# An attention and MLP kernel on one core: some thirty words of a hand-written step table change places

## The chip, the cores and the metric

The kernel runs on one core of a Trainium2 chip. The metric is the device time of one execution in microseconds (us), as the median of three runs. A second number, the span, comes from one further execution that the hardware profiler recorded: it is the stretch from the first to the last instruction of the program in the trace.

## The reference

The input is q, k and v of shape (8 batches, 8 heads, 576 positions, 64), s of shape (8, 8, 576), a gain of 512 numbers and two weight matrices. Everything is float32 outside the kernel.

```python
cum = np.cumsum(np.maximum(s, 0.0), axis=-1)
bias = -(cum[:, :, :, None] - cum[:, :, None, :])
scores = np.where(causal, -1e9, scale * (q @ k.T) + np.minimum(bias, 0.0))
attn = softmax(scores)                     # over the last axis
x = (attn @ v)  ->  (batch, 576, 512)      # the heads side by side
xn = (x - mean(x)) / np.sqrt(var(x) + 1e-6) * g_ln
out = x + np.maximum(xn @ w_ch1, 0.0) @ w_ch2   # 512 -> 2048 -> 512
```

So there are eight batches of causal attention whose scores carry a decay bias, and behind each a layer norm and a two-layer MLP with a residual.

## The kernel before

**The table.** All of the work is done in `fast_path`. Its last part is a table of words, `PLAN` (line 1317), and a loop that takes the words one after the other, looks each up in the dictionary `STEPS` and calls the step, which emits its instructions. A word is a step's name, its arguments behind dots, and at times an engine behind a colon (A is ScalarE, D is VectorE, P is GpSimd). Each engine works off its own instructions strictly in the order in which the words emitted them, so the place of a word decides what an instruction stands behind on its engine. Words that go to different engines only wait for each other's data and buffers. DMAs are issued by an engine as well: those of SyncE (SP in the profile) go out on its hardware queue (q1), those of GpSimd (POOL), which cast float32 to bfloat16 on the way, on a software queue (q0). A GpSimd DMA uses one of eight semaphores in turn, so that issue n waits until DMA n-8 has landed.

**The work on TensorE (PE).** Batch 0 is done tile by tile. Batch 1 is done head by head: `s.8` to `s.15` are its scores (line 391), `v.8` to `v.15` its products with v (`pv`, line 590), where each word takes all five key blocks of one head. From batch 2 on two heads go together: `B2.n` (`burst`, line 553) makes the scores of pair n, `bx` their exponentials on ScalarE (line 560), `bm` the causal masks on GpSimd (`select`, line 497), and `Y` (`pv_two`, line 626) the products. The MLP of each batch is a queue of units from which `u` and `U` take the next one and put it between the attention: first the 16 units of the first layer (`ph`, line 792), then for each of four row tiles four quarters of the second layer (`py`, line 811), of which quarter i needs quarter i of the second weight matrix. Behind the fourth quarter the result goes out (`yo`, line 823, output DMA line 844).

**What is loaded where.** The names in the prediction are these:
- On GpSimd's queue: `w1.c` and `w2.i` load a quarter of the first and the second weights (lines 253 and 256, 512 KB each, tile `w_bf`). `lp.g` loads the k and the q of head pair g (`kp`, `qp`, line 184, 144 KB each); pair 7 is the last of batch 1, which has pairs 4 to 7, and pair 8 is the first of batch 2. `LV.b.t` loads a block of v (line 192, 128 KB, the last block 64 KB).
- On SyncE's queue: `lr.b.t` loads the rows of k and of q of a batch and row block as float32 (line 206, `rowtmp`, 256 KB each), `lv.b.t` the rows of v. `aug` and `a3` copy the bias rows into the key and query tiles of batches 0 and 1 (lines 265 and 267). `D` is the DMA that transposes the normed rows of batch 1 for its MLP (line 763), `Da.1.4` the one for the last, short row blocks of batches 0 and 1 (line 759), whose MLP units come at the very end of the queue, `tr` transposes k and q rows (line 225).
- On GpSimd's compute queue: `cr.b.t.u` casts a loaded row tile (line 218), `vm.b.t:P` multiplies v rows with the key weights (line 233), `vo` writes the weights' own columns (lines 245 and 246), `tk` copies the tail keys (line 145), `bm` are the masks.
- On TensorE and behind it: `Q` transposes a loaded pair (line 323) and `E` copies it out, `F` and `G` do so for the pairs of batch 2 (line 361), `l` is the last step of the layer norm of batch 1 (`xn`, line 741, VectorE).

The weight quarters, pairs and v blocks all stand in one row on GpSimd's queue. The rows for later batches stand in one row on SyncE's. The two queues use the same sixteen DMA engines of the core.

Of the kernel before, what the change touches and what calls it, by code (L numbers as in the profile page):

```python
# [16 lines left out]
P = 128  # L17
# [13 lines left out]
def fast_path(  # L31
# [13 lines left out]
    B, H, S, D = q.shape  # L45
# [13 lines left out]
    G = 4  # L59
# [896 lines left out]
    E = {"A": "act", "D": "dve", "P": "pool", "S": "sync"}  # L956
# [249 lines left out]
    def raise_flag(count, ones, n):  # L1206
# [113 lines left out]
        lc.k.3 lc.q.3 g LV.0.2 w1.0 LV.0.3 lp.4 cr2.0 cr2.1 fv.1 fk.0 fk.1 lc.k.4 lc.q.4 w1.1 f.7 f.8 fv.0 lp.5  # L1320
        w1.2 f.9 f.10 LV.1.0 LV.1.1 LV.1.2 LV.1.3 LV.1.4 lp.6 LV.0.4 w1.3 w2.0 lp.7 lp.8 w2.1 f.11 relu.0 scan.0
# [3 lines left out]
        x.1.1.0 T.2.1 e.2.0:D S.1.0.1 lr.3.0 lp.9 x.1.0.0 V.1.1 x.1.0.1 S.2.0.1 e.2.1:D S.2.0.2 S.2.1.2 T.3.0  # L1325
        S.2.1.1 N.1.1 S.2.0.0 L.0 V.1.0 x.2.0.1 x.2.0.2 x.2.1.2 X.0 e.3.0:D N.1.0 x.2.1.1 L.1 x.2.0.0 S.2.1.0
        S.3.0.2 B.0.1 T.3.1 B.1.0 x.2.1.0 e.3.1:D B.1.1 S.3.0.0 S.3.0.3 y.0:A aug x.3.0.2 V.2.0 M.0.0.0 x.3.0.3
        M.0.0.3 S.3.0.1 V.2.1 S.3.1.1 x.3.0.1 N.2.0 M.0.0.2 bc.4 S.3.1.3 x.3.0.0 X.1 x.3.1.3 y.1:A N.2.1 M.0.0.1
        S.3.1.2 V.3.0 S.3.1.0 M.0.1.3 L.2 T.4.0 M.0.1.0 r.0.0:A N.3.0 X.2 x.3.1.2 Q.q.4 x.3.1.0 x.3.1.1 e.4.0:D
        T.4.1 y.2:D M.0.1.2 Q.k.4 E.q.4.0:A B.3.0 E.k.4.0:A S.4.0.1 e.4.1:D S.4.1.0 M.0.1.1 E.q.4.1:D E.k.4.1:D  # L1330
        x.4.0.1 x.4.1.0 U A.1 V.3.1 s.8 N.3.1 u L.3 B.2.1 B.2.0 d.8 S.4.0.0 X.3 y.3:A r.0.1:D Q.q.5 E.q.5.1:A
        E.q.5.0:D S.4.1.1 x.4.1.1 x.4.0.0 Q.k.5 Sk u wr u u v.8 La.3 E.k.5.0:D B.3.1 n.8 B.0.0 U xk cr.3.0.0 a3
        lr.3.1 Q.k.6 E.k.6.0:A E.k.5.1:A u s.9 V.4.1 E.k.6.1:D N.4.1 M.0.2.3 M.0.2.2 V.4.0 Q.q.6 N.4.0 s.10 v.9
        A.3 qu.3 M.0.2.0 lp.11 d.10 A.2 M.0.2.1 E.q.6.0:D s.11 n.9 u Q.k.7 E.q.6.1:D w2.2 d.12 s.12 r.0.2:A
        E.k.7.0:D E.k.7.1:D O2.k.8:A v.10 n.10 Q.q.7 u s.13 E.q.7.0:D w2.3 E.q.7.1:D wT v.11 lp.10 u wx n.11
        ga.1.0.2 lv.2.0 A.0 u d.14 ga.1.0.0 v.12 qu.4 n.12 O2.k.9:A s.14 cr.3.1.0 ga.1.0.3 u F.k.8 v.13 u R qu.5
        n.13 La.6 F.k.9 ga.1.1.2 s.15 v.14 u G.k.9:D ga.1.1.0 n.14 U v.15 O2.q.8:A O2.q.9:A U n.15 F.q.9 qu.6
        lr.3.2 O2.k.11:A vo.2:P u ga.1.2.0 ga.1.2.1 ga.1.0.1 La.2 me cr.3.1.1 u l.0 O2.q.11:A F.q.8 U ga.1.1.3
# [280 lines left out]
```

## Time and profile before

| | us |
|---|---|
| median of three runs | 345.14 |
| lowest and highest of these | 344.15, 345.18 |
| the profiled execution's own time | 346.36 |
| its span | 344.9 |
| its time outside the span | 1.46 |
| PE busy | 331.5 (96% of the span) |
| VectorE, ScalarE, GpSimd busy | 199.5, 187.7, 168.6 |

The profile lists times in us from the start of the span. PE is TensorE's matmuls, DVE is VectorE, ACT is ScalarE, POOL is GpSimd, and SPq is the time in which SyncE issued a DMA. A row of the timeline gives the start, the duration, the engine, the line, the operation, what it writes and reads (tile names without their numbers), how many instructions the row holds, and in brackets how long the engine stood before it and what ended that. A row of the DMA view gives for each queue the number of packets, the MB moved and the share of the engines' time. TensorE was granted 0.991 of its full clock.

### The profile page before, as it was taken

Reading aid. Unit: us, or ns where it says so; the run is one execution under the profiler, and the core shown is the slowest. Engines: PE = TensorE matmul, PEld = TensorE weight load, DVE = VectorE, ACT = ScalarE, POOL = GpSimd, SP = SyncE. Lnnn points to the kernel's source line nnn. Section 1 sums busy time; section 2 is a strip of 40 time slices with the busy share of each in tenths; the row PEclk is TensorE's granted clock in tenths of the full one; section 3 lists DMA queues with packets and bytes.
Section 4 is the critical chain, followed back from the end, with each engine's and each line's share of the span. In section 5 each row is a group of like instructions: output and inputs, shape, how many; then the busy total and the mean of one; then the engine's idle time right before and its main releaser. Section 6 shows DMA issues by size and latency. Waiting matters only on the chain.

```text
span 344.9 us, 8061 instructions
## 1 busy us (share of the span) xinstructions
PE 331.5 (96%) x3117; PEld 183.3 (53%) x3117; DVE 199.5 (58%) x567; ACT 187.7 (54%) x348; POOL 168.6 (49%) x305
## 2 busy tenths in 40 slices
PE   6999989989998998999999999999999999999993
PEld 2899756545554554555555545554455444444443
DVE  6598777837685675347653664566448624523421
ACT  4998899677664675357736774486344204202200
POOL 8896768777377947683984377441301001000000
PEclk9899999999999999999999999999999999999998
DMA  9999999999999999999998966700510141020022
GB/s 144 181 189 177 172 193 195 214 208 233 164 215 227 169 245 195 216 228 198 205 209 205 214 108 151 139 2 2 121 63 2 24 129 46 3 90 33 2 62 65
DMA packets 147962, 48.59 MB, mean 141 GB/s; under 512 B 135280, under 2 KB 143760, under 8 KB 147920
## 3 DMA queue, kind: packets, MB, share of 16 engines
q1 hardware_dynamic: 121856, 38.34, 57.3%
q0 software_dynamic: 24304, 8.92, 22.0%
q10 hardware_dynamic: 1760, 0.79, 0.9%
q8 instruction: 25, 0.41, 0.5%
q14 instruction: 17, 0.14, 0.1%
HBM read 37.11 MB, written 9.44 MB: 135 GB/s over the span
## 4 chain that ended last, share of the span: by engine, by line
PE 77%; DMA 10%; POOL 7%; DVE 1%; issue 1%; SPq 1%; ACT 0%; POOLq 0%; DVEq 0%
PE py L811 34%; PE ph L792 31%; DMA v_bf<-in_v_dram 5%; PE pot L626 4%; DMA kp<-in_k_dram 3%; PE sa L553 2%; DMA rowtmp<-in_k_dram 2%; PE sb L553 1%; PE sc L553 1%; PE pott L664 1%; DMA rowtmp<-in_v_dram 1%; POOL rowb L180 1%; PE pot L590 1%; SPq L206 1%; POOL v_bf L233 1%
## 5 line engine op out<-in xcount | busy, mean ns | idle before, releaser
L811 PE MATMUL py<-w_bf,hT 128*128 128x512 bf16 (+2 forms) x608 | 131.1, 368 | 0.1
L792 PE MATMUL ph<-xT,w_bf 128*128 128x512 bf16 x480 | 109.8, 379 | 0.2 <-ACT er L560 0.2
L783 ACT ACTIVATE hT<-ph 128x512 bf16<-128x512 f32 x102 | 60.9, 604 | 77.6 <-PE ph L792 76.1
L811 PEld LDWEIGHTS <-hT 128*128 128x128 bf16 x608 | 55.9, 98 | 59.8
L792 PEld LDWEIGHTS <-w_bf 128*128 128x128 bf16 x544 | 51.3, 98 | 56.5 <-issue 0.3
L497 POOL TENSOR_SCALAR_AFFINE_SELECT er<-er 128x256 bf16<-128x256 bf16 x96 | 38.8, 419 | 48.7 <-ACT er L560 34.3
L823 DVE SCALAR_TENSOR_TENSOR yo<-py,rstd,xb 128x512 f32<-128x512 f32 x32 | 24.0, 751 | 50.5 <-PE py L811 46.2
L560 ACT ACTIVATE er<-sb 128x512 bf16<-128x512 f32 x48 | 28.2, 609 | 22.1 <-PE sb L553 17.9
L781 DVE TENSOR_SCALAR hT<-ph 128x512 bf16<-128x512 f32 x34 | 23.5, 691 | 27.5 <-PE ph L792 26.0
L233 POOL TENSOR_TENSOR v_bf<-rowtmp,wt 128x512 bf16<-128x512 f32 (+1 forms) x30 | 33.1, 1107 | 10.0 <-DMA rowtmp<-in_v_dram 9.8
L560 ACT ACTIVATE er<-sa 128x512 bf16<-128x512 f32 x48 | 28.6, 609 | 16.4 <-PE sa L553 15.1
L560 ACT ACTIVATE er<-sc 128x512 bf16<-128x512 f32 x48 | 28.8, 614 | 3.8 <-PE sc L553 3.8
L626 PEld LDWEIGHTS <-er 128*128 128x128 bf16 x480 | 19.8, 97 | 12.8 <-POOL er L497 4.0
L715 POOL TENSOR_TENSOR rstd<-rstd,mhalf 128x4 f32<-128x4 f32 (+1 forms) x8 | 8.7, 1093 | 34.3 <-DVE rstd L714 34.2
L626 PE MATMUL pot<-v_bf,er 128*128 128x66 bf16 x480 | 22.5, 193 | 3.1 <-POOL er L497 2.1
L700 DVE BATCH_NORM_STATS2 stats<-xb 128x6 f32<-128x128 f32 (+1 forms) x84 | 24.8, 326 | 0.6
L741 DVE SCALAR_TENSOR_TENSOR xn<-xb,mv,gb 128x512 bf16<-128x512 f32 x28 | 24.5, 874 | 1.0
L218 POOL CAST kq<-rowtmp 128x512 bf16<-128x512 f32 (+1 forms) x30 | 19.0, 645 | 12.2 <-DMA rowtmp<-in_k_dram 11.8
L643 DVE TENSOR_REDUCE sums<-pot 128x4 f32<-128x8 f32 x48 | 7.8, 163 | 29.5 <-PE pot L626 29.1
L645 DVE TENSOR_TENSOR xb<-pot,rinvs 128x256 f32<-128x256 f32 x48 | 20.4, 424 | 1.7
L553 PEld LDWEIGHTS <-kq 64*128 64x128 bf16 x384 | 11.9, 94 | 9.6 <-issue 4.2
L218 POOL CAST rowb<-rowtmp 128x512 bf16<-128x512 f32 (+1 forms) x20 | 12.8, 652 | 3.3 <-DMA rowtmp<-in_k_dram 2.9
(178 smaller groups left out, 393.2 us busy)
## 6 DMA issues: line engine op xcount, KB each, us to landing
out_dram<-yo SPq DMA_DIRECT2D x32, 256.0 KB
rowtmp<-in_v_dram SPq DMA_DIRECT2D x24, 256.0 KB
rowtmp<-in_k_dram SPq DMA_DIRECT2D x20, 256.0 KB
rowtmp<-in_q_dram SPq DMA_DIRECT2D x20, 256.0 KB
w_bf<-in_moe_w_ch_dram POOLq DMA_DIRECT2D x8, 512.0 KB, 9.0
kp<-in_k_dram POOLq DMA_DIRECT2D x8, 144.0 KB, 10.2
qp<-in_q_dram POOLq DMA_DIRECT2D x8, 144.0 KB, 10.2
v_bf<-in_v_dram POOLq DMA_DIRECT2D x8, 128.0 KB, 8.3
```

The lines of the kernel that those rows point to most:

```text
L218: nc.gpsimd.tensor_copy(out=rows[b % 2][0:pn, t, u], in_=loaded.pop(("kq"[u], b, t))[0:pn])
L233: e.tensor_tensor(out=v_bf[b % 2][0:pn, t, :, 0:D], in0=loaded.pop(("v", b, t))[0:pn], in1=wt[0:pn, t, b, :].unsqueeze(2).to_broadcast([pn ...
L497: nc.gpsimd.affine_select(out=out, in_=out, compare_op=ALU.is_ge, fill=0.0, base=0, pattern=pattern, channel_multiplier=-1,)
L553: nc.tensor.matmul(a, lhsT=lhsT, rhs=rhs, start=True, stop=True)
L560: nc.scalar.activation(out=er[:, 2 * n % 4 + i, o : o + 512], in_=bank["B", n].pop((name, i)), func=ACT.Exp, scale=scale,)
L626: nc.tensor.matmul(pot[:, t, :], lhsT=e[:, o : o + P], rhs=v_bf[b % 2][:, kb, h, :], start=(kb == 0), stop=(kb == t),)
L700: nc.vector.bn_stats(out=st[b][:, t, part, :], in_=x_tiles(b)[t][:, lo:hi])
L741: nc.vector.scalar_tensor_tensor(out=xn, in0=tiles[t], scalar=mvs[b][:, t, 0:1] if b > 0 else mean0[:, t : t + 1], in1=gb, op0=ALU.subtrac ...
L783: nc.scalar.activation(out=dst, in_=ph, func=ACT.Relu)
L792: nc.tensor.matmul(ph, lhsT=w1_bf[:, kd, fb * P : (fb + 1) * P], rhs=xT[:, :, kd, :], start=(kd == 0), stop=(kd == KD - 1),)
L811: nc.tensor.matmul(py[t], lhsT=hT[:, fb, t * P : (t + 1) * P], rhs=w2_bf[:, fb, c0:c1], start=(fb == 0), stop=(fb == FB - 1),)
L823: nc.vector.scalar_tensor_tensor(out=yo, in0=py[t], scalar=rs, in1=x[:, c0:c1], op0=ALU.mult, op1=ALU.add)
```

## The change

The table is written in another order. No word goes and none is new; one word, `r.0.2`, names VectorE instead of ScalarE. Nothing outside the table changes. The first rows that differ:

```diff
-        w1.2 f.9 f.10 LV.1.0 LV.1.1 LV.1.2 LV.1.3 LV.1.4 lp.6 LV.0.4 w1.3 w2.0 lp.7 lp.8 w2.1 f.11 relu.0 scan.0
+        f.9 f.10 LV.1.0 LV.1.1 LV.1.2 LV.1.3 fk.0 LV.1.4 lp.6 LV.0.4 lp.7 lp.8 w1.3 w2.0 f.11 relu.0 scan.0
...
-        B.0.0 U xk cr.3.0.0 a3
-        lr.3.1 Q.k.6 E.k.6.0:A E.k.5.1:A u s.9
+        B.0.0 U xk cr.3.0.0 lr.3.1 a3 Q.k.6 E.k.5.1:A E.k.6.0:A E.k.6.1:D u s.9
```

(The second pair is cut to the words around the move.) In the order of the program:

1. **GpSimd's loads.** `lp.7` and `lp.8` go ahead of `w1.3` and `w2.0`, and `w2.1` goes behind `lp.9`. A small memset (`fk.0`) goes behind `LV.1.3`.
2. **SyncE's first rows.** `lr.3.1` goes ahead of `a3`.
3. **Small steps between 30 and 62 us.** `E.k.5.1` goes ahead of `E.k.6.0` on ScalarE, `r.0.2` goes to VectorE, and `v.14` goes ahead of `s.15` on TensorE.
4. **Around the start of batch 2.** `lv.2.3` and `lv.2.4` go ahead of `lr.3.3`; `l.1` and `D` go back, `D` behind `lr.3.4` and a second output; `cr.3.0.1` and `cr.3.2.0` go ahead of `vo.3`; `vm.2.1` goes ahead of `tk.2`; `F.q.11`, `G.q.9` and `bx.9.2` go forward and `O2.k.10` back.
5. **Later.** `cr.4.1.0` goes behind the mask `bm.12.0`, `cr.5.1.0` and `cr.5.0.0` behind the mask `bm.16.2`; `Da.1.4` goes back behind `lr.5.2`; `lr.6.0` goes ahead of `lr.5.4`, and `lv.6.0` behind `lv.5.4`.

On SyncE, in the first fifteen of its DMAs, this is what changes (`kq_111` and `kq_110` are the key and query tiles of batches 0 and 1 that get the bias rows, from `aug` and `a3`):

```order
 L265 DMA kq_111<-c_122 1x4x576
 L267 DMA kq_111<-c_122 1x4x576 x3
+L206 DMA rowtmp<-in_k_dram 128x8x64
+L206 DMA rowtmp<-in_q_dram 128x8x64
 L265 DMA kq_110<-c_122 1x4x576
 L267 DMA kq_110<-c_122 1x4x576 x3
-L206 DMA rowtmp<-in_k_dram 128x8x64
-L206 DMA rowtmp<-in_q_dram 128x8x64
 L206 DMA rowtmp<-in_v_dram 128x8x64
```

The two row loads of `lr.3.1` now stand ahead of the four copies of `a3`.

On GpSimd, in the row of its early loads, the pairs and the weights change places (the first pair of the piece is pair 7, the second pair 8; line 253 is `w1.3`, the first row of line 256 is `w2.0`):

```order
 L192 DMA v_bf_107<-in_v_dram 64x8x64
-L253 DMA w_bf<-in_moe_w_ch_dram 128x4x512
-L256 DMA w_bf<-in_moe_w_ch_dram 128x4x512
-L184 DMA kp<-in_k_dram 96x2x384
-L184 DMA qp<-in_q_dram 96x2x384
-L184 DMA kp<-in_k_dram 96x2x384
-L184 DMA qp<-in_q_dram 96x2x384
+L184 DMA kp<-in_k_dram 96x2x384
+L184 DMA qp<-in_q_dram 96x2x384
+L184 DMA kp<-in_k_dram 96x2x384
+L184 DMA qp<-in_q_dram 96x2x384
+L253 DMA w_bf<-in_moe_w_ch_dram 128x4x512
```

Four loads of 144 KB now stand ahead of two of 512 KB; the row that follows, line 256, is `w2.0` in both.

On GpSimd again, at the first pair of batch 4 (`er` are the exponentials that the masks cut, `kq_111` takes the cast rows of batch 5, `v_bf` the weighted v rows):

```order
 L233 TENSOR_TENSOR v_bf_107<-rowtmp,wt 64x8x64
-L497 AFFINE_SELECT er<-er 128x2x128 x3
-L218 CAST kq_111<-rowtmp 128x512 x2
-L497 AFFINE_SELECT er<-er 128x2x128
-L218 CAST kq_111<-rowtmp 128x512 x2
+L497 AFFINE_SELECT er<-er 128x2x128 x4
+L218 CAST kq_111<-rowtmp 128x512 x4
 L233 TENSOR_TENSOR v_bf_108<-rowtmp,wt 128x8x64
```

The fourth mask (`bm.16.2`) no longer stands behind two casts.

More of the change, by code (lines that the diff above doesn't have):

```diff
@@ L1324, in fast_path @@
         V.0.1 N.0.1 tc.2 e.1.0:A S.1.0.0 e.1.1:A S.1.1.1 x.0.0.0 x.1.1.1 qu.2 V.0.0 S.1.1.0 bc.2 T.2.0 N.0.0
[L1325 to L1338, printed above, removed]
@@ new lines, in fast_path @@
+        S.2.1.0 S.3.0.2 B.0.1 T.3.1 B.1.0 x.2.1.0 e.3.1:D B.1.1 S.3.0.0 S.3.0.3 y.0:A aug x.3.0.2 V.2.0 M.0.0.0
+        x.3.0.3 M.0.0.3 S.3.0.1 V.2.1 S.3.1.1 x.3.0.1 N.2.0 M.0.0.2 bc.4 S.3.1.3 x.3.0.0 X.1 x.3.1.3 N.2.1
+        M.0.0.1 y.1:A S.3.1.2 V.3.0 S.3.1.0 M.0.1.3 L.2 T.4.0 M.0.1.0 r.0.0:A N.3.0 X.2 x.3.1.2 Q.q.4 x.3.1.0
+        x.3.1.1 e.4.0:D T.4.1 y.2:D M.0.1.2 Q.k.4 E.q.4.0:A B.3.0 E.k.4.0:A S.4.0.1 e.4.1:D S.4.1.0 M.0.1.1
+        E.q.4.1:D E.k.4.1:D x.4.0.1 x.4.1.0 U A.1 V.3.1 s.8 N.3.1 u L.3 B.2.1 B.2.0 d.8 S.4.0.0 X.3 y.3:A
@@ new lines, in fast_path @@
+        u F.k.8 v.13 u R qu.5 n.13 La.6 F.k.9 ga.1.1.2 v.14 s.15 u G.k.9:D ga.1.1.0 n.14 U v.15 O2.q.8:A
+        O2.q.9:A U n.15 F.q.9 qu.6 lr.3.2 O2.k.11:A vo.2:P u ga.1.2.0 ga.1.2.1 ga.1.0.1 La.2 me cr.3.1.1 u l.0
+        O2.q.11:A F.q.8 U ga.1.1.3 ga.1.1.1 lv.2.1 lv.2.2 G.k.8:A ga.1.2.2 vm.2.0:P ga.1.2.3 lv.2.3 lv.2.4
+        lr.3.3 F.q.11 l.3 F.k.11 u G.q.9:A cr.3.0.1 l.2 G.q.8:A cr.3.2.0 vo.3:P G.k.11:A G.q.11:D lr.3.4 u U
+        O2.k.10:A l.1 D F.k.10 U O2.q.10:A G.k.10:A F.q.10 vm.2.1:P to G.q.10:A u lv.3.0 U lr.4.0 tk.2 B2.8
@@ new lines, in fast_path @@
+        vm.2.2:P bx.8.3 u bx.8.1 vm.2.3:P sd.2 bx.8.4 vm.2.4:P bx.8.2 qu.7 se.2 u bx.8.5 sm.2 ga.1.0.4 u bx.8.0
+        bm.8.3 u bm.8.1 B2.9 bx.9.2 bm.8.2 bm.8.0 bx.9.5 Y.8.1 ga.1.1.4 lr.4.1 cr.3.2.1 bx.9.4 cr.3.3.0 bx.9.0
+        Y.8.0 cr.3.3.1 K.8.0 tr.3.0.2 bm.9.3 cr.3.4.1 K.8.1 bm.9.0 bx.9.3 bx.9.1 bm.9.1 u bm.9.2 U u u Y.9.0
+        vm.3.0:P ga.1.2.4 la.1.4 B2.10 bx.10.0 K.9.0 bx.10.3 bx.10.4 bx.10.2 bx.10.5 cr.3.4.0 bm.10.3 bx.10.1
+        Y.9.1 U K.9.1 u tr.3.2.4 u U u lv.3.1 tr.3.4.5 bm.10.1 Y.10.1 bm.10.0 B2.11 bx.11.0 bx.11.4 lv.3.2
@@ new lines, in fast_path @@
+        bx.11.5 lv.3.3 K.10.1 bm.10.2 Y.10.0 K.10.0 bm.11.2 ga.2.0.0 lv.3.4 bx.11.2 bm.11.0 La.4 bx.11.1 u
+        ga.2.1.2 ga.2.0.3 U u cr.4.1.1 lr.4.2 bx.11.3 Y.11.0 K.11.0 bm.11.3 u U bm.11.1 u ga.2.0.1 lr.4.3
+        cr.4.0.1 vm.3.1:P Y.11.1 K.11.1 lv.4.0 lv.4.1 tk.3 vm.3.4:P lr.4.4 u ga.2.1.0 u Z.2 z.2 B2.12 bx.12.0
+        vm.3.2:P U bx.12.4 bm.12.2 ga.2.1.1 bx.12.1 lv.4.2 ga.2.2.0 cr.4.2.1 ga.2.2.1 ga.2.1.3 lv.4.3 la.2.0
+        la.2.1 cr.4.0.0 bx.12.5 bm.12.3 vm.3.3:P ga.2.2.2 bx.12.3 bm.12.1 u bx.12.2 bm.12.0 cr.4.1.0 u u sd.3
@@ new lines, in fast_path @@
+        se.3 u B2.13 bx.13.5 bx.13.1 ga.2.0.2 la.2.2 u bx.13.0 cr.4.4.0 sm.3 u bx.13.4 ga.2.2.3 u la.2.3 Da.2.0
+        bx.13.3 u Y.12.0 bx.13.2 bm.13.0 K.12.0 u u B2.14 cr.4.4.1 tr.4.4.5 bx.14.2 Y.12.1 K.12.1 bx.14.1
+        bm.13.2 bx.14.3 vo.4:P bx.14.4 u u u tr.4.0.2 bx.14.5 bm.13.1 bm.13.3 bx.14.0 Y.13.0 B2.15 bx.15.0
+        K.13.0 bx.15.2 cr.4.3.1 cr.4.2.0 cr.4.3.0 tr.4.2.4 u lr.5.0 u vm.4.1:P Y.13.1 bx.15.3 bx.15.5 bx.15.1 u
+        K.13.1 bx.15.4 bm.14.1 bm.14.2 bm.15.0 tk.4 ga.3.0.0 U U bm.14.0 u bm.15.1 Y.14.0 K.14.0 bm.14.3 Y.14.1
@@ new lines, in fast_path @@
+        cr.5.4.0 u cr.5.4.1 bx.17.2 bx.17.3 bm.17.0 la.3.1 la.3.2 la.3.3 cr.5.2.0 bm.17.1 tr.5.4.5 bx.17.5
+        bm.17.3 lr.6.1 u u qm u u cr.5.3.1 u cr.5.2.1 u tk.5 vo.5:P cr.6.1.1 Da.3.0 u u lv.5.4 Y.17.0 lv.6.0
+        B2.18 bx.18.3 bx.18.2 bx.18.0 K.17.0 bx.18.1 u u Y.17.1 K.17.1 bx.18.4 bx.18.5 bm.18.3 tr.5.2.4 u u
+        ga.3.1.4 ga.3.0.4 B2.19 bx.19.0 vm.5.3:P bx.19.3 bm.18.2 ga.4.0.1 bm.18.1 cr.5.0.1 bm.18.0 tr.5.0.2
+        vm.5.0:P bx.19.1 u bm.19.1 u u lv.6.1 sd.5 u bx.19.5 se.5 Y.18.1 sm.5 K.18.1 u vm.5.1:P Y.18.0 ga.3.2.4
@@ new lines, in fast_path @@
+        u la.5.3 Da.5.0 cr.7.3.1 bm.25.1 u u u u cr.7.2.0 B2.26 bx.26.3 bm.25.0 vm.7.2:P bx.26.4 Y.25.0 bx.26.2
+        K.25.0 cr.7.2.1 bx.26.1 bm.26.2 u u u bm.25.3 Y.25.1 bx.26.0 bx.26.5 K.25.1 ga.6.0.0 vm.7.3:P bm.26.0
+        B2.27 bx.27.0 u tk.7 bx.27.4 sd.7 bx.27.3 bm.27.2 bx.27.5 u ga.6.0.3 u bm.26.3 bm.26.1 se.7 la.5.4
+        tr.7.2.4 u u U Y.26.1 u U sm.7 bx.27.1 bm.27.1 Da.5.4 Y.26.0 K.26.0 bm.27.3 K.26.1 ga.6.1.2 bx.27.2
+        bm.27.0 vm.7.4:P ga.6.1.3 u vm.7.1:P u u Y.27.0 K.27.0 ga.6.1.0 Z.6 z.6 B2.28 bx.28.0 ga.6.0.2 bx.28.1
@@ new lines, in fast_path @@
+        bm.30.1 U u U bm.30.3 bx.31.1 bm.31.1 Y.30.1 K.30.1 ga.7.1.0 bm.31.3 ga.7.1.3 bx.31.4 bm.31.2 u U Y.31.1
+        K.31.1 U bm.31.0 ga.7.1.2 u Y.31.0 K.31.0 u Z.7 z.7 ga.7.2.2 ga.7.2.3 ga.7.2.0 u ga.7.0.4 ga.7.1.4
+        ga.7.2.4 ga.7.1.1 u u u U ga.7.0.0 u u u u la.7.0 ga.7.2.1 la.7.1 la.7.2 la.7.3 Da.7.0 u u u u u u u u u
+        u u u u u u u u U u U u la.7.4 U u U u u u u U U gd u Da.7.4 u u u u u u u u u u u u u u u u U u u u U U
+        U u u U u U U U U fl u u u u u u vl u u u u u u u u u u u u u u u u u u
```

92 lines of the change are left out of this document (33 added, 59 removed).

## The prediction

> **What bounds the kernel now.** The page comes first. TensorE is busy nearly throughout.
>
> ```profile
> span 344.9 us, 8061 instructions
> PE 331.5 (96%) x3117; PEld 183.3 (53%) x3117; DVE 199.5 (58%) x567; ACT 187.7 (54%) x348; POOL 168.6 (49%) x305
> ```
>
> No instruction of TensorE is added or dropped, so the time can change only through the 344.9 − 331.5 = 13.4 us in which it stands, or through new standing. The timeline of PE, read next, shows where it stands once the start is over. The brackets give how long and behind what.
>
> ```profile
> 45.11 0.43 PE L323 MATMUL trqk<-ident,kp 96*128 96x96 bf16 x6 [0.98 <-DMA kp<-in_k_dram]
> ...
> 74.94 0.48 PE L626 MATMUL pot<-v_bf,er 128*128 128x66 bf16 x10 [0.75 <-POOL er L497]
> 75.65 0.48 PE L626 MATMUL pot<-v_bf,er 128*128 128x66 bf16 x10 [0.24 <-POOL er L497]
> ...
> 105.96 0.48 PE L626 MATMUL pot<-v_bf,er 128*128 128x66 bf16 x10 [1.00 <-DVE rstd L714]
> ...
> 131.63 0.33 PE L626 MATMUL pot<-v_bf,er 128*128 128x66 bf16 x5 [1.13 <-POOL er L497]
> ```
>
> These five stalls add up to 0.98 + 0.75 + 0.24 + 1.00 + 1.13 = 4.10 us, and the change touches what stands behind each of them. That is the most that it can gain. Whether it gains it depends on a limit that these rows don't show: how much the DMA engines move. I read that from the DMA view (packets, MB, share of the engines), first from 22.5 to 30.5 us, where GpSimd's queue q0 runs alone, then from 37.7 to 62 us, where SyncE's queue q1 runs beside it.
>
> ```profile
> q0 software_dynamic: 2884, 1.50, 140.2%
> q1 hardware_dynamic: 6, 0.00, 0.1%
> DMA packets 2890, 1.51 MB, mean 188 GB/s; under 512 B 1501, under 2 KB 2890, under 8 KB 2890
> ...
> q0 software_dynamic: 4188, 3.61, 92.3%
> q1 hardware_dynamic: 3806, 0.97, 29.7%
> DMA packets 7997, 4.62 MB, mean 190 GB/s; under 512 B 4016, under 2 KB 7994, under 8 KB 7994
> ```
>
> Alone, q0 gets 188 GB/s. With q1 beside it both together get 190, and q0 is left with 3.61 MB / 24.3 us = 149. The sum stays, so what q1 moves is taken from q0. Until 62 us TensorE is fed by q0.
>
> **Part 1, SyncE's rows ahead of a3.** The timeline of SyncE shows the copies of `aug` (18.27), then `a3` (32.85 and after), then the two loads of `lr.3.1`.
>
> ```profile
> 18.27 1.95 SPq L267 DMA_DIRECT2D kq<-c  x3
> 32.85 0.57 SPq L265 DMA_DIRECT2D kq<-c  x1
> 33.48 1.81 SPq L267 DMA_DIRECT2D kq<-c  x3
> 35.33 0.47 SPq L206 DMA_DIRECT2D rowtmp<-in_k_dram  x1
> 35.84 0.82 SPq L206 DMA_DIRECT2D rowtmp<-in_q_dram  x1
> ```
>
> SyncE stands from 20.2 to 32.85 because `a3` overwrites a tile that TensorE still reads. While it stands, q0 has the engines to itself. `lr.3.1` has fresh buffers and nothing to wait for, so ahead of `a3` it goes out at about 20.2, 15 us sooner, and its 2 x 256 KB = 0.524 MB move in the very stretch in which q1 moved nothing. `a3` itself still goes out at 32.85; nothing else is queued behind the early rows. What q0 carries there is late by 0.524 MB / 190 GB/s = 2.8 us. The first to feel it is `v.8`, which needs the last v block of batch 1:
>
> ```profile
> 24.46 4.22 POOL L192 DMA_DIRECT2D v_bf<-in_v_dram  x5
> v_bf<-in_v_dram POOLq DMA_DIRECT2D x1, 64.0 KB, 7.9
> 35.32 0.78 PE L590 MATMUL pot<-v_bf,er 128*128 128x65 bf16 x15
> ```
>
> The fifth issue of the first row goes out at about 27.9 and lands 7.9 later (second row, from the DMA view of that moment), at 35.8. `v.8` runs from 35.32 to 36.10, so it has no slack, and TensorE stands for some 2.8 us there.
>
> **Part 2, the pairs ahead of the weights.** The chain of waits of before runs through pair 7:
>
> ```profile
> 35.09 9.98 DMA kp<-in_k_dram
> ```
>
> The load stands behind `w1.3` and `w2.0` and lands at 45.07, which makes the stall of 0.98 at 45.11. Ahead of two loads of 512 KB it lands far sooner, even 2.8 us delayed, and the stall goes. The weights come later by the four pair loads only, covered by the units on `w1.2` that run first; should that cover be gone, TensorE would stand sooner, but within the wait that the last quarter sets anyway. For the total of bytes ahead of the last weight quarter, `w2.3`, is the same in both orders, and at that quarter q0 lets TensorE go:
>
> ```profile
> 50.99 0.76 POOL L256 DMA_DIRECT2D w_bf<-in_moe_w_ch_dram  x1
> w_bf<-in_moe_w_ch_dram POOLq DMA_DIRECT2D x1, 512.0 KB, 11.5
> 62.59 1.03 PE L811 MATMUL py<-w_bf,hT 128*128 128x512 bf16 x4
> ```
>
> It is issued at 50.99, lands 11.5 later at 62.5, and the fourth quarter of the first row tile starts at 62.59: slack 0.1. So the pair's 0.98 alone is worth 0.1. With 0.524 MB more ahead of it, `w2.3` lands later by 0.524 / 190 = 2.8 (if q1 runs dry for it later) to 0.524 / 149 = 3.5 (if q1 keeps its share). q1 has work waiting most of the time, so I take 3.3. TensorE then starts this quarter at 65.8 instead of 62.59: **+3.2** (2.7 to 3.5). The stall of `v.8` lies inside this and isn't added.
>
> The Trainium skill, page "DMA: Bandwidth & Descriptors", section "Anatomy of one DMA", fits a GpSimd DMA by 2.0 us plus its bytes over 436 GB/s; by that the 0.524 MB would cost 1.2 us, and the sum below would end 2.0 us lower, at 343.5. The measured 188 and 190 GB/s speak against it.
>
> **Part 3, around batch 2's start.** GpSimd's timeline gives the stalls at 74.94 and 75.65:
>
> ```profile
> 71.18 1.04 POOL L233 TENSOR_TENSOR v_bf<-rowtmp,wt 128x512 bf16<-128x512 f32 x1 [1.60 <-DMA rowtmp<-in_v_dram]
> 72.51 1.03 POOL L233 TENSOR_TENSOR v_bf<-rowtmp,wt 64x512 bf16<-64x512 f32 x1 [0.29 <-DMA rowtmp<-in_v_dram]
> ...
> 74.12 1.47 POOL L497 TENSOR_SCALAR_AFFINE_SELECT er<-er 128x256 bf16<-128x256 bf16 x4
> ```
>
> The masks stand behind two multiplications that wait 1.60 and 0.29 us for v rows, together more than the 0.99 of both stalls. The change loads these rows ahead of `lr.3.3` and takes `vm.2.1` out from behind the tail keys. With TensorE 3.2 us later as well, the masks are there first. **−0.99.** The other small moves up to here (`E`, `r.0.2`, `v.14`, `F`, `G`, `bx.9.2`) change places on ScalarE, VectorE and GpSimd, which are idle for about half of the span by the page's first rows, and I cost them at nothing; ahead of `w2.3` a wait that one of them made would lie inside the 3.2, behind it the wait would be added.
>
> **Part 4, casts behind masks.** At 105.96 the releaser named is VectorE, but the mask is the one that ends last, at 105.90. These rows are GpSimd's and then VectorE's:
>
> ```profile
> 102.77 0.40 POOL L497 TENSOR_SCALAR_AFFINE_SELECT er<-er 128x256 bf16<-128x256 bf16 x1
> ...
> 104.13 0.60 POOL L218 CAST rowb<-rowtmp 128x512 bf16<-128x512 f32 x1
> 104.69 1.21 POOL L497 TENSOR_SCALAR_AFFINE_SELECT er<-er 128x256 bf16<-128x256 bf16 x2
> ...
> 104.52 1.11 DVE L741 SCALAR_TENSOR_TENSOR xn<-xb,mv,gb 128x512 bf16<-128x512 f32 x1
> ```
>
> Without the cast of 0.60 in between, two masks of 0.40 from 104.1 on end at 104.9, just when TensorE is free (105.96 − 1.00 = 104.96): a gain up to 1.0. But a mask and the `xn` of VectorE ran long together (1.21 for two instead of 0.80, 1.11), and may again: then only 0.3 is won. I take **−0.7**, nearer to the end without the collision, since the masks now start ahead of `xn`.
>
> The page "SBUF — State Buffer" of the Trainium skill, section "Who interferes with whom", says that a VectorE operation and one of GpSimd can lock each other out of a shared port for a whole instruction, by which the second mask would wait out `xn` and the gain would be the 0.3; the sum would then end at 345.9.
>
> At 131.63 the mask stands behind casts whose rows are late:
>
> ```profile
> 130.05 1.16 POOL L218 CAST kq<-rowtmp 128x512 bf16<-128x512 f32 x2 [2.32 <-DMA rowtmp<-in_k_dram]
> 131.17 0.41 POOL L497 TENSOR_SCALAR_AFFINE_SELECT er<-er 128x256 bf16<-128x256 bf16 x1
> ```
>
> GpSimd waited 2.32 us here with the mask queued behind. Put first, the mask ends before 130, and TensorE doesn't wait: **−1.13**. The casts come no later by it, since their rows set them; `Da.1.4`, moved back, is wanted by the last units of the queue only.
>
> **The sum.** +3.2 − 0.99 − 0.7 − 1.13 = +0.4. Bounds: 2.7 − 0.99 − 1.0 − 1.13 = −0.4 and 3.5 − 0.99 − 0.3 − 1.13 = +1.1. The profiled execution took 346.36, of which the change makes 346.8; that run lies 1.2 above the median of 345.14, and against the median I forecast **345.5**, in this case 344.7 to 346.2.
>
> **Rivals.** *Faster: the early rows cost q0 nothing that TensorE feels.* If the engines have room that q0 alone can't use, or q1's early bytes are made good later (0.524 MB less stand in q1 after 35 us), `w2.3` lands when it did. Then −0.1 − 0.99 − 0.7 − 1.13 = −2.9, 342.2; with 1.2 us of delay 343.5. For it: in later slices of the page the queues together reach 233 GB/s. Against it: 188 and 190 in the two stretches that count, 24 us long.
>
> *Slower: the transposed rows of batch 1 come after TensorE wants them.* `D` now stands behind two more row loads and an output on SyncE, and one of these loads needs the buffer that `vm.2.1` frees on GpSimd.
>
> ```profile
> 69.84 3.06 SPq L763 DMA_TRANSPOSE xT<-xn  x1
> 73.01 0.65 SPq L206 DMA_DIRECT2D rowtmp<-in_k_dram  x1
> 73.76 0.59 SPq L206 DMA_DIRECT2D rowtmp<-in_q_dram  x1
> 74.44 0.58 SPq L844 DMA_DIRECT2D out_dram<-yo  x1
> ...
> 75.97 2.32 PE L792 MATMUL ph<-xT,w_bf 128*128 128x512 bf16 x10
> ```
>
> Before, its issue ended at 72.90, and 3.07 us later TensorE used the rows without a wait. Three more issues (0.65 + 0.59 + 0.58) put it to 74.7; TensorE comes 3.2 − 0.99 = 2.2 later, at 78.2, so an issue that ends by 75.1 is surely in time. If the loads and the output move with TensorE, it ends at up to 74.7 + 2.2 = 76.9, and the wait is up to 1.8: 345.5 + 1.8 = 347.3, with 1.6 as my value 347.1. It decides when the issue of `D` ends later than about 75.1. For it: nearly no work between can fill the gap. Against it: 3.07 holds unknown slack, and `lr.3.1` is out of SyncE's way.
>
> **Numbers.** Chances: forecast 0.50, faster rival 0.27, slower rival 0.23. A measurement can tell about 0.3%, 1.04 us, from no change. Of the forecast's case, 344.7 to 346.2, nearly all lies within that; I count 0.42 for it, 0.07 above and 0.01 below. So faster 0.28, same 0.42, slower 0.30. The range takes in the forecast's case, the better half of each rival's and what lies between: 342.2 to 347.2.
>
> **What would show it.** In the changed profile `lr.3.1` is issued near 20, q1 moves some 0.5 MB before 35 us, a stall of 2 to 3 us stands ahead of `v.8`, and the stall at pair 7 is gone. The first fourth quarter of `py` starts near 65.8. The waits at 74.94 and 131.63 are gone and that at 105.96 is small. No wait for `xT` stands at the first `ph` of batch 1; if it does, the slower rival is right. If `v.8` runs at 35.3 as before, my account of the shared engines is wrong, and the time is near 342.2.

## The result, and the profile after

| | us |
|---|---|
| the kernel before, median of 7 runs | 344.10 (343.04 to 345.18) |
| the changed kernel, median of 7 runs | 346.73 (345.44 to 347.76) |
| ratio, 95% interval | 1.0068 (1.0041 to 1.0095) |
| span of the profiled execution, before and after | 344.9, 343.9 |

The change makes the kernel slower by 0.7%, 1.4 to 3.3 us. The two traces alone say the opposite: the profiled execution of the changed kernel is 1.0 us shorter than that of before. It took 345.44 us, the fastest of its seven; that of before took 346.36, more than any of its seven timed runs. Each trace thus comes from an edge of its kernel's spread, and this matters below.

The page of the changed kernel, span and busy times, to be held against the first rows of before:

```profile
span 343.9 us, 8062 instructions
PE 331.0 (96%) x3117; PEld 182.4 (53%) x3117; DVE 199.3 (58%) x568; ACT 187.2 (54%) x347; POOL 168.0 (49%) x305
```

SyncE's timeline after. The two loads of `lr.3.1` go out at 19.9 and 20.4, and `a3` follows at 32.62:

```profile
17.93 1.95 SPq L267 DMA_DIRECT2D kq<-c  x3
19.93 0.44 SPq L206 DMA_DIRECT2D rowtmp<-in_k_dram  x1
20.43 0.57 SPq L206 DMA_DIRECT2D rowtmp<-in_q_dram  x1
32.62 0.59 SPq L265 DMA_DIRECT2D kq<-c  x1
```

The DMA view after, 22.5 to 30.5 us (queue, packets, MB, share of the engines). SyncE's q1 moves 0.38 MB where it moved nothing, and GpSimd's q0 moves 1.22 MB instead of 1.50:

```profile
q0 software_dynamic: 1421, 1.22, 93.4%
q1 hardware_dynamic: 1476, 0.38, 30.9%
DMA packets 2898, 1.61 MB, mean 201 GB/s; under 512 B 1619, under 2 KB 2897, under 8 KB 2897
```

TensorE's timeline after. The first two rows are `v.8`, the next two the third and the fourth quarter of the first row tile; the last is the first `sd` of batch 2, which I use as a mark:

```profile
36.57 0.28 PE L590 MATMUL pot<-v_bf,er 128*128 128x65 bf16 x4 [0.99 <-DMA v_bf<-in_v_dram]
37.77 0.64 PE L590 MATMUL pot<-v_bf,er 128*128 128x65 bf16 x6 [0.91 <-DMA v_bf<-in_v_dram]
...
62.02 1.02 PE L811 MATMUL py<-w_bf,hT 128*128 128x512 bf16 x4 [0.35 <-DMA w_bf<-in_moe_w_ch_dram]
...
65.51 2.96 PE L811 MATMUL py<-w_bf,hT 128*128 128x512 bf16 x12 [0.84 <-DMA w_bf<-in_moe_w_ch_dram]
...
73.28 0.40 PE L524 MATMUL sd<-kq,c 128*128 128x64 bf16 x8
```

`v.8` waits for v blocks, the stall at pair 7 is gone, and the last weight quarter sets the start of the fourth quarter at 65.51. Behind it, no wait at 75, 106 or 131 us is left. All steps of the prediction can be seen, but the time isn't what they summed up to.

### The profile page after: what moved, and what is told of

The parts are those of the page before. It is cut to its first block, busy times and chain, and to the rows that moved or that the text cites. A ratio compares the mean times of both kernels' runs of the same rounds, so it can differ in the third digit from the quotient of the medians.

```text
span 343.9 us, 8062 instructions
## 1 busy us (share of the span) xinstructions
PE 331.0 (96%) x3117; PEld 182.4 (53%) x3117; DVE 199.3 (58%) x568; ACT 187.2 (54%) x347; POOL 168.0 (49%) x305
## 4 chain that ended last, share of the span: by engine, by line
PE 82%; DMA 9%; POOL 5%; issue 1%; ACT 1%; DVE 0%; POOLq 0%; DVEq 0%; ACTq 0%
PE py L811 35%; PE ph L792 33%; DMA v_bf<-in_v_dram 5%; PE pot L626 4%; DMA w_bf<-in_moe_w_ch_dram 4%; PE sa L553 2%; PE sb L553 1%; PE sc L553 1%; PE pott L664 1%; POOL v_bf L192 1%; POOL rowb L180 1%; POOL w_bf L253 1%; POOL kq L951 1%; DVE yo L823 0%; ACT er L402 0%
## 5 line engine op out<-in xcount | busy, mean ns | idle before, releaser
L497 POOL TENSOR_SCALAR_AFFINE_SELECT er<-er 128x256 bf16<-128x256 bf16 x96 | 38.1, 411 | 53.7 <-ACT er L560 39.2
L218 POOL CAST kq<-rowtmp 128x512 bf16<-128x512 f32 (+1 forms) x30 | 19.7, 674 | 9.0 <-DMA rowtmp<-in_k_dram 9.0
L645 DVE TENSOR_TENSOR xb<-pot,rinvs 128x256 f32<-128x256 f32 x48 | 20.4, 425 | 1.7
L792 PE MATMUL ph<-xTm,w_bf 128*128 128x512 bf16 x64 | 14.0, 379 | 0.0
```

Source lines behind the costliest of these rows:

```text
L497: nc.gpsimd.affine_select(out=out, in_=out, compare_op=ALU.is_ge, fill=0.0, base=0, pattern=pattern, channel_multiplier=-1,)
L792: nc.tensor.matmul(ph, lhsT=w1_bf[:, kd, fb * P : (fb + 1) * P], rhs=xT[:, :, kd, :], start=(kd == 0), stop=(kd == KD - 1),)
```

## The experiments

The theory: early rows on SyncE's queue take engine time from GpSimd's queue and hold TensorE at the weight quarters; the rest gains or is free. The rivals: the order of GpSimd's loads, or the moves behind 62 us, are to blame.

**One: the changed kernel with the rows put back (e1).**

```diff
-xk cr.3.0.0 lr.3.1 a3 Q.k.6
+xk cr.3.0.0 a3 lr.3.1 Q.k.6
```

> The changed kernel with one word put back: lr.3.1 behind a3 on SyncE. Theory one (the early rows take 0.52 MB from GpSimd's queue and so hold TensorE at the first row tile's fourth quarter, and all other moves gain or are free): faster than the changed kernel by 2 to 3 us, thus 343.7 to 344.7 against 346.7, no stall ahead of v.8, the last weight quarter landing near 62.5. It is also faster than before if the stalls at 75, 106 and 131 us that the trace of before shows are in most of its executions (then about 341.5), and equal to before (344) if they are not. Theory two (the slowdown comes from the pairs ahead of the weights, or from the moves behind 62 us): within 0.5 us of the changed kernel.

Measured: 344.21 against 343.39 for before, ratio 1.0021 (0.9995 to 1.0046). The changed kernel stood at 1.0068, so the rows cost some 0.5%, 1.6 us (by the two intervals roughly 0.3 to 2.9), less than I had expected. Whether this is all of the loss can't be told, since the interval of this run takes in 1; nothing is gained over before. Another part of the expectation failed: without any early rows `v.8` still waits 0.61 + 0.41 us for v blocks in this trace. The traces of e3 and e7 have no such wait.

**Two: the kernel before with the rows alone (e2).**

```diff
-a3 lr.3.1
+lr.3.1 a3
```

> The kernel before with one move: lr.3.1 ahead of a3 on SyncE. Theory one: v.8 stalls for 2 us and the fourth quarter starts near 65.5 instead of 62.6, so slower than before by 2.0 to 3.2 us (346.1 to 347.3), less what the later stalls give back because GpSimd's work then comes in time. Theory two: within 0.5 us of before.

Measured: 345.58, ratio 1.0061 (1.0032 to 1.0089), 2.1 us slower. TensorE's timeline shows the wait at `v.8` and, since the pairs stand behind the weights here, a longer one at pair 7:

```profile
37.35 0.25 PE L590 MATMUL pot<-v_bf,er 128*128 128x65 bf16 x3 [0.71 <-DMA v_bf<-in_v_dram]
38.42 0.28 PE L590 MATMUL pot<-v_bf,er 128*128 128x65 bf16 x4 [0.82 <-DMA v_bf<-in_v_dram]
39.00 0.41 PE L590 MATMUL pot<-v_bf,er 128*128 128x65 bf16 x6 [0.30 <-DMA v_bf<-in_v_dram]
49.27 0.43 PE L323 MATMUL trqk<-ident,kp 96*128 96x96 bf16 x6 [1.83 <-DMA kp<-in_k_dram]
```

One swap of two words thus makes a loss as large as that of the whole change. The trace, though, is that of the slowest of its twelve runs, 348.60 us against the median of 345.58. In it the first fourth quarter starts at 68.38 and not near the 65.5 that I expected, because the wait at pair 7 comes on top, and because TensorE's granted clock is only 0.60 from 51 to 55 us, behind that wait (experiment six comes back to this).

**Three: the kernel before with GpSimd's loads alone (e3).**

```diff
-LV.0.4 w1.3 w2.0 lp.7 lp.8 w2.1 ... lp.9
+LV.0.4 lp.7 lp.8 w1.3 w2.0 ... lp.9 w2.1
```

(`fk.0` moves too.)

> The kernel before with the GpSimd loads of the changed kernel and nothing else (pairs 7 and 8 ahead of two weight quarters, a third quarter behind pair 9, the memset later). Theory one: the stall of 0.98 us at pair 7 goes, but the last weight quarter still lands near 62.5, so the time moves by no more than 0.5 us. Theory two, the form in which this order is to blame: slower than before by 2 us or more.

Measured: 342.77, ratio 0.9988 (0.9959 to 1.0018): no change that can be told. But its trace corrects my reasoning, below.

**Four: the moves behind 62 us and the small steps alone (e4).** The changed kernel, with both edits above undone. It also holds a small step that the list of the change leaves out: `y.1`, on ScalarE, goes two words back.

> The changed kernel with both early moves undone (lr.3.1 behind a3, GpSimd's loads in the order of before); what is left are the small steps and the moves behind 62 us. Theory one: faster than before by up to 2.8 us if the stalls at 75, 106 and 131 us are in most executions of before, by 0 to 1 us if the trace of before caught a bad execution. Theory two, the form in which the later moves are to blame: slower than before by 2 us.

Measured: 343.82, ratio 1.0006 (0.9981 to 1.0032). So they are not to blame for a loss of 2 us, and neither do they gain what I had put down for them. One reason stands in TensorE's timeline, the first unit of batch 1's MLP:

```profile
76.53 3.63 PE L792 MATMUL ph<-xT,w_bf 128*128 128x512 bf16 x16 [1.35 <-DMA xT<-xn]
```

This is my slower rival, the transposed rows that come too late. In the changed kernel TensorE is so late that this wait doesn't show; e1 has it too, with 0.58 us.

**Five: e4 with `l.1`, `O2.k.10` and `D` put back (e5).**

```diff
-lr.3.4 u U O2.k.10:A l.1 D F.k.10
+O2.k.10:A D lr.3.4 u U F.k.10
```

(`l.1` goes back behind `lv.2.1`.)

> The run with the later moves alone (e4), with l.1, O2.k.10 and the transposing DMA D put back to where they stood before. Theory one (with TensorE not held up by late weights, D behind two more loads and an output is late, as e4's wait of 1.35 us for xT shows): the wait for xT goes, and the time falls by 0.7 to 1.4 us against e4, to about 0.2 to 0.3% below before. Rival (the wait for xT only takes the place of a wait that comes anyway): the same as e4 and as before, within 0.5 us.

Measured: 342.96 against 343.58, ratio 0.9980 (0.9960 to 0.9999). The wait for `xT` is gone. It is 0.26% below e4, about 0.9 us, though the two intervals overlap. It is the only version whose interval leaves out 1 on the fast side, at 0.2% below before; among ten versions one that just does so may be chance.

**Six: the changed kernel with twice the early rows (e6).**

```diff
-lr.3.1 a3
+lr.3.1 lr.3.2 a3
```

> The changed kernel with twice the early rows: lr.3.2 goes ahead of a3 too, so 1.05 MB stand in SyncE's queue at 20 us instead of 0.52. Theory one (what SyncE's queue moves early is taken from GpSimd's queue): all loads of GpSimd behind it are late by 2.8 to 3.5 us more until the early rows are through, v.8 stalls for some 4 us in all, and the time rises by 1.5 to 3 us against the changed kernel, some 1.2 to 1.5% above before; less if the queue of SyncE, now emptier later, gives part back by the last weight quarter. Rival (the early loads are harmless, something else costs): within 0.5 us of the changed kernel.

Measured: 349.29, ratio 1.0173 (1.0140 to 1.0206), 3.6 us above the changed kernel's 1.0068: more than expected. `v.8` now waits 1.03 + 1.90 + 0.55 + 0.43 = 3.9 us:

```profile
36.95 0.25 PE L590 MATMUL pot<-v_bf,er 128*128 128x65 bf16 x3 [1.03 <-DMA v_bf<-in_v_dram]
39.10 0.28 PE L590 MATMUL pot<-v_bf,er 128*128 128x65 bf16 x4 [1.90 <-DMA v_bf<-in_v_dram]
39.93 0.31 PE L590 MATMUL pot<-v_bf,er 128*128 128x65 bf16 x5 [0.55 <-DMA v_bf<-in_v_dram]
40.67 0.21 PE L590 MATMUL pot<-v_bf,er 128*128 128x65 bf16 x1 [0.43 <-DMA v_bf<-in_v_dram]
```

Why it is more than expected can be seen right behind this wait. The granted clock is 0.57 from 40 to 44 us, and the four matmuls of a unit take 1.89 us; in e2's trace four such matmuls, at 46.42 and ahead of its slow stretch, take 1.03.

```profile
40.70 1.89 PE L792 MATMUL ph<-xT,w_bf 128*128 128x512 bf16 x4
```

A clock of 0.57 for 4 us is 1.7 us of work lost. In the changed kernel's trace TensorE stands for 2.0 us in all between 35 and 39 us, and its clock stays at 1.00. So of the 3.6 us some 1.9 are the longer wait and some 1.7 the clock, an estimate from one trace of each.

**Seven: the changed kernel with the rows and `D` both put back (e7).** The edits of e1 and e5 together.

> The changed kernel with both suspects put back: lr.3.1 behind a3, and l.1, O2.k.10 and D where they stood before. What is left are the pairs ahead of the weights, the v loads ahead of rows, the casts behind masks and the small steps. Theory one: no stall ahead of v.8 beyond chance, none for xT; the wait for the last weight quarter stays at about 1 us. So 0.2 to 0.5% faster than before (0.7 to 1.7 us), and faster than the changed kernel by 2.5 to 3.5 us. Rival (a part of the loss lies in the moves that are left): the same as before or slower.

Measured: 343.52, ratio 0.9987 (0.9964 to 1.0010). With these two moves undone the loss is gone: the ratio is 0.0081 below that of the changed kernel, 2.8 us, as expected. A gain over before, which I had expected too, can't be told; its trace still waits 0.58 and 0.75 us for weight quarters.

**Eight: e7 with fewer bytes ahead of `w2.3` (e8).**

```diff
-M.0.2.0 lp.11 d.10 ... w2.3 E.q.7.1:D wT v.11 lp.10
+M.0.2.0 d.10 ... w2.3 lp.11 E.q.7.1:D wT v.11 lp.10
-lr.3.2 O2.k.11:A vo.2:P ... l.0 O2.q.11:A F.q.8 ... G.k.8:A ga.1.2.2
+lr.3.2 vo.2:P ... l.0 F.q.8 ... G.k.8:A O2.k.11:A O2.q.11:A ga.1.2.2
```

> e7 with 0.29 MB fewer ahead of the last weight quarter on GpSimd's queue: the loads of pair 11 go behind w2.3, and its two copies on ScalarE behind G.k.8. Theory one (bytes ahead of w2.3 in both queues set when the fourth quarter of the first row tile starts): w2.3 lands 1.5 to 2 us sooner, its wait of about 1 us goes, and the time falls by up to 1.1 us against e7, 0.4 to 0.8% below before. Rival (the copies of pair 11 then come late and TensorE waits for its transposes instead): within 0.5 us of e7 or slower, with a wait at line 361.

Measured: 346.10 against 343.58, ratio 1.0075 (1.0045 to 1.0104): the rival. ScalarE's and then TensorE's timeline:

```profile
61.32 0.83 ACT L141 COPY rowb<-kp 96x768 bf16<-96x768 bf16 x1 [2.62 <-DMA kp<-in_k_dram]
...
63.75 1.07 PE L361 MATMUL trp<-ident,rowb 96*128 96x96 bf16 x12 [2.04 <-ACT kq L141]
```

ScalarE stands 2.62 us ahead of a copy whose load comes late, with another copy queued behind it that TensorE needs. A load put later takes along whatever is queued behind its reader. The clock adds to it here too: it is 0.57 from 64 to 68 us, and twelve matmuls take 4.35 us that take 2.96 in the changed kernel (its row at 65.51):

```profile
64.61 4.35 PE L811 MATMUL py<-w_bf,hT 128*128 128x512 bf16 x12
```

Of the twelve timed runs of e8, the six with a mean granted clock of 0.990 or less have a median of 347.7 us, the six above it 345.3.

**Nine and ten: the same with the readers moved too, on e7 (e9) and on e3 (e10).** The copies of pair 11 go behind those out of pair 8, its transposes two units later.

```diff
-F.q.11 l.3 F.k.11 u G.q.9:A cr.3.0.1 l.2 G.q.8:A
+l.3 u G.q.9:A cr.3.0.1 l.2 G.q.8:A O2.k.11:A O2.q.11:A
-cr.3.2.0 vo.3:P G.k.11:A G.q.11:D O2.k.10:A D lr.3.4 u U F.k.10
+cr.3.2.0 vo.3:P D lr.3.4 u F.k.11 U F.q.11 G.k.11:A G.q.11:D O2.k.10:A F.k.10
```

> e7 once more with the loads of pair 11 behind w2.3, but now its copies on ScalarE stand behind the copies out of pair 8 and its transposes on TensorE two units later, so that nothing is queued behind the late pair (in e8 a copy was, and TensorE waited 2.04 us at line 361 for it). Theory one: w2.3 lands near 60.2 as in e8, the waits for the weight quarters that e7 shows (0.58 and 0.75 us) go, none comes at line 361, and the time falls by 0.8 to 1.3 us against e7, 0.4 to 0.7% below before. Rival (TensorE is held by something that comes right behind, such as the next pair's transposes): within 0.5 us of e7.

> The same on the basis of e3 (the kernel before with the GpSimd loads of the changed kernel alone). Theory one: the waits of e3 for the weight quarters (0.17 and 0.96 us) go, and the time falls by 0.6 to 1.1 us against e3, 0.4 to 0.6% below before. Rival: within 0.5 us of e3.

Measured: e9 343.40 against 343.74, ratio 1.0008 (0.9985 to 1.0031); e10 344.39, ratio 0.9999 (0.9970 to 1.0028). The waits for weights are gone, the time stays, against the expectation of both. In e10's trace the waits at 105 and 131 us are there, with 0.85 and 0.90 us, that e3's trace doesn't have. In e9 TensorE comes earlier to the next row tile and waits for VectorE to empty its bank:

```profile
64.47 1.02 PE L811 MATMUL py<-w_bf,hT 128*128 128x512 bf16 x4 [0.96 <-DVE yo L823]
```

**Eleven and twelve: the kernel before, unchanged, for two more traces.**

> The kernel before, unchanged, for a second trace. Theory one in its present form (the stalls at 75, 106 and 131 us of the first trace are no fixed part of the kernel, since that execution was 2 to 3 us slower than the median): at most one of the three stalls is there again, the wait for pair 7 near 45 us is there again with 0.3 to 1 us. Rival (they are fixed, and the later moves of the change did remove them but something else took the gain): all three are there again with about 1 us each.

> The kernel before, unchanged, for a third trace; the same expectations as for the second.

Measured: one execution each, 343.61 and 344.54. TensorE's waits between 33 and 135 us in the second trace:

```profile
73.29 0.47 PE L626 MATMUL pot<-v_bf,er 128*128 128x66 bf16 x10 [0.32 <-POOL er L497]
74.01 0.48 PE L626 MATMUL pot<-v_bf,er 128*128 128x66 bf16 x10 [0.24 <-POOL er L497]
129.22 0.33 PE L626 MATMUL pot<-v_bf,er 128*128 128x66 bf16 x5 [1.26 <-POOL er L497]
```

and in the third:

```profile
104.32 0.48 PE L626 MATMUL pot<-v_bf,er 128*128 128x66 bf16 x10 [0.85 <-DVE rstd L714]
130.17 0.33 PE L626 MATMUL pot<-v_bf,er 128*128 128x66 bf16 x5 [1.30 <-POOL er L497]
```

My expectation was wrong in both halves. The stall at 131 is there in all three traces of before, that at 106 in two with some size, that at 75 in two; the wait for pair 7, which I had called the fixed one, is in neither (e4, with the same order of loads, has it with 0.72).

## Why the prediction was right and wrong

346.73 lies in the range and the mechanism was named, but the likeliest case, no change that can be told, didn't come. The range is 5 us wide and takes in three outcomes, so lying in it says little. That 346.73 is only 1.2 us above the forecast of 345.5 is in part luck: the median of three runs on which the forecast stood, 345.14, is 1.0 above the 344.10 of seven runs. As a difference, +0.4 was forecast and +2.6 came. One step of the working was wrong, several terms were off in size, and the base on which all of them stood was not that of a median execution.

**The base.** I read all stalls of before from one trace as if each execution had them. Three traces of before, cut at the first `sd` of batch 2 (70.44, 69.22, 69.99 us), and the changed kernel (73.28):

| | start to mark | mark to end |
|---|---|---|
| before, first trace (span 344.9) | 70.4 | 274.5 |
| before, second (342.1) | 69.2 | 272.9 |
| before, third (343.0) | 70.0 | 273.0 |
| changed (343.9) | 73.3 | 270.6 |

Against the first trace the change loses 2.8 ahead of the mark and wins 3.8 behind it (274.46 − 270.62). Against the other two it loses 3.3 to 4.1 and wins 2.3 to 2.4, by the spans +0.9 (343.9 − 343.0) to +1.8 (343.9 − 342.1), with the changed kernel in its fastest execution, 1.3 us below its median. The mean of +0.9 and +1.8 and these 1.3 add up to 2.6, the difference of the two medians. The forecast was +3.2 and −2.8; the cost was booked too low by about 0.5, the gain too high by about 0.4, and the rest is how far the changed kernel's trace lies below its median. What fills these 1.3 us no trace shows. The clock may have a part in it: the traced execution had a mean granted clock of 1.000, while four of the seven timed runs had 0.987, and none of the 87 timed runs of before that lie beside the experiments is below 0.989. But the clock doesn't put the seven in order, for the one with 0.999 took 347.10.

**Part 1, the early rows: right in place, too large in size.** The row loads leave at 20 us, q1 takes 0.38 MB in the 8 us shown, and `v.8` waits 0.99 + 0.91 us and some more, though e1 shows that a wait of 1.0 can stand there without the rows. The mark of the changed kernel lies 2.5 behind that of e1 (73.28 − 70.81), which differs from it by this one word; it lies 2.6 and 1.7 behind those of e3 and e7, and `w2.3` lands 1.8 to 2.7 later than in these three. e2 has 2.1 us for this move alone (1.1 to 3.1). The forecast had 2.7 to 3.5. It said that the sum of both queues stays, so that what q1 moves is taken from q0. But with both queues busy the engines moved 201 GB/s in the 8 us shown, against 188 with one, and q0 lost 0.28 MB (1.50 − 1.22) where q1 gained 0.38, about three quarters; in e2 it lost 0.40 for 0.50. Three quarters of the 2.8 us are 2.1, an estimate that fits the runs. The 1.2 us that came out of the Trainium skill's fit (page "DMA: Bandwidth & Descriptors", section "Anatomy of one DMA") lies below all of these values, though inside the interval of e2.

**Part 2, the pairs: wrong.** The step that failed reads "the total of bytes ahead of the last weight quarter, `w2.3`, is the same in both orders". So it is, but the queue ran short of bytes on the way. GpSimd's issue of `w1.3`, then the DMA view from 36 to 42 us (q0 and q1), in the second trace of before:

```profile
31.45 0.77 POOL L253 DMA_DIRECT2D w_bf<-in_moe_w_ch_dram  x1 [0.16 <-issue]
...
q0 software_dynamic: 1142, 1.05, 106.6%
q1 hardware_dynamic: 507, 0.14, 16.4%
```

and the same in e3, with the issue of `w2.3`, its time to landing and TensorE's wait for it:

```profile
36.14 0.79 POOL L253 DMA_DIRECT2D w_bf<-in_moe_w_ch_dram  x1
...
q0 software_dynamic: 863, 0.68, 79.1%
q1 hardware_dynamic: 1976, 0.51, 41.0%
...
50.18 0.77 POOL L256 DMA_DIRECT2D w_bf<-in_moe_w_ch_dram  x1
w_bf<-in_moe_w_ch_dram POOLq DMA_DIRECT2D x1, 512.0 KB, 12.6
...
62.85 1.02 PE L811 MATMUL py<-w_bf,hT 128*128 128x512 bf16 x4 [0.95 <-DMA w_bf<-in_moe_w_ch_dram]
```

GpSimd has eight semaphores for its DMAs and waits for the eighth last to land. With the small pair loads first, the eight that are under way hold fewer bytes, and the big loads are issued 4.7 us later. q0 moves 0.68 MB in place of 1.05, q1 takes the gap, and `w2.3` lands at 62.8. In the second trace of before it lands sooner:

```profile
50.15 0.77 POOL L256 DMA_DIRECT2D w_bf<-in_moe_w_ch_dram  x1
w_bf<-in_moe_w_ch_dram POOLq DMA_DIRECT2D x1, 512.0 KB, 10.6
```

That is 60.75, 2 us earlier. The other traces agree. With the loads in the order of before and no early rows (three of before, e4 and e5), q0 moves 0.98 to 1.06 MB in these 6 us and `w2.3` lands between 60.7 and 62.5; with the pairs first and no early rows (e1, e3, e7), it moves 0.66 to 0.68 MB and `w2.3` lands between 62.8 and 63.7. In time this order costs nothing that can be told (e3); it also spares pair 7's wait where there is one, and no wait for masks is left in e3's trace. But in the changed kernel the fourth quarter waits for `w2.3` until 65.5, so that it lands 4.75 later than in this trace of before (3.0 to 4.8 later than in the five), and not 3.3: part of it is the rows', part the short queue's. That the small loads are the cause is read from the traces; no run has the pairs first and the queue kept full.

**Part 3, the masks at 75: open.** The stalls are gone in the changed kernel, but the three traces of before have 0.99, 0.56 and none, and e2, e3 and e10, which have none of the later moves, have no wait there either. What the move is worth is not shown.

**Part 4, the casts: right at 131 where the wait comes.** No trace of a kernel with the casts behind the mask `bm.16.2` (the changed one, e1, e4 to e9) has the wait at 131. Of the six with the old order, the three of before have it, with 1.13, 1.26 and 1.30, and e10 with 0.90; e2 and e3 don't. So the −1.13 fits an execution that has the wait. That at 106 was 1.00, at most a tenth, and 0.85 in the traces of before, for which I took 0.7. But e5 and e9 have 0.57 and 0.25 there in spite of the move, with VectorE as releaser. e2 and e3 lack both waits without any of the moves. In e2 TensorE is 6 us later; why e3 lacks them, I don't know.

**The slower rival: real, but hidden.** It costs TensorE 1.35 us in e4 and 0.58 in e1 and nothing in the changed kernel. With `D` moved back, and `l.1` and `O2.k.10` with it, e5 and e7 have no such wait.

What stays open: why executions of one kernel differ by 4 us (before: 341.51 to 345.52 in 35 runs), and so how much of the 2.3 us belongs to each part in a median execution.

## What to carry to other kernels

A queue that stands blocked may be the reason why another has the DMA engines to itself; a load moved ahead of the blockage is then paid for by the other queue, which here lost about three quarters of the bytes that the first one gained, so ask who needs the bytes that it displaces. When issues are bounded in number, small loads ahead of big ones can leave the queue short of bytes, even if the sum of bytes is the same. Before stalls of a trace are added up as a gain, look whether that execution's time is near the median: here it was 2.3 us above it, and more traces would have shown which stalls are always there. A stall can also cost more than its length, when the clock falls behind it.

## What the runs showed of the hardware

**Two queues.** With both queues full the engines took packets from them in nearly equal number, whatever their size. In the changed kernel from 46 to 60.5 us:

```profile
q0 software_dynamic: 2459, 2.21, 91.8%
q1 hardware_dynamic: 2339, 0.59, 30.8%
```

That is 2459 and 2339 packets, but 2.21 and 0.59 MB. The Trainium skill, page "DMA: Bandwidth & Descriptors", section "Queues, rings and completion order", says that each engine takes turns between its queues packet by packet. This trace agrees as far as it goes, with 1.05 packets of q0 for each of q1; the page's packet is a run of several descriptors, and no run here shows whether the profile counts the same thing. In e1, e3, e4 and e7 the two numbers of this stretch, some 2440 to 2470, differ by 4 at most. Where q0 was short, from 36 to 42 us in e3, they were 863 and 1976. So with both queues full a queue's share of the bytes follows from the size of its packets: the row loads, at 0.59 MB in 2339 packets some 250 bytes each, get a fifth of the bytes.

**The clock behind a wait.** In three of the fourteen traces the granted clock falls to 0.50 in the middle of the kernel, each time behind a long wait of TensorE: 1.83 us in e2, 3.9 us in four pieces in e6, 2.04 us in e8. Each time 1.7 us of work are lost, which at 0.50 is some 3.4 us of time. The other eleven have no wait of TensorE longer than 1.35 us in one piece between 12 and 338 us, and no clock below 0.99 there. No run varies the length of a wait alone, so where the limit lies is not shown.
